# Skewing eight attention heads by a stage in the start of a fused attention and mixture-of-experts kernel

## The chip, the core and the metric

The kernel runs on one core of one Trainium2 chip. The metric is the device time of one execution in microseconds (us). TensorE (PE) multiplies; VectorE (DVE), ScalarE (ACT) and GpSimd (POOL) work on what it leaves; the DMA transfers are issued from one queue, that of SyncE (SP). Each engine takes its instructions in the order in which the program gives them and waits at the first whose inputs are missing.

## The reference

Attention with a decay in the scores, followed by a dense mixture of four experts over all tokens. Batch 4, 8 heads, 576 positions, head size 64; 2304 tokens, model size 512, hidden size 1024.

```python
scores = scale * (q @ k.T)                       # per head
cum = np.cumsum(np.log(np.clip(f, 1e-4, 1)), -1)
scores = where(causal, -1e9, scores + cum[..., :, None] - cum[..., None, :])
attn = softmax(scores)
x = (attn @ v)  ->  tokens x 512
p = domain_probs / domain_probs.sum(-1)
out = sum over e of p[:, e] * (relu(x @ w1[e]) @ w2[e])
```

## The kernel before

Every matrix product is made of float32 operands split into a high part (a float32r copy, written `hi`, `th`, `wh`) and a low part (the rest, `kl`, `tl`, `wl`), so each split costs one copy and one subtraction, and each product two or three passes of TensorE.

The positions of a batch are cut into a first half of 256 rows and a second of 320. A `Job` is one batch, one pair of heads and one half; a head of a job is what the loops run over. The tokens are cut into nine chunks of 256. The experts run as `Step`s, each with a chunk and two 128-wide pieces of a hidden layer; a step needs two weight tiles of 128 x 1024. In the first sweep the first eight steps all use chunk 0, so each of them wants two new weight tiles.

Chunk 0 needs the first halves of all eight heads of batch 0. They are worked in `startup()`, under a manual schedule: the order of the calls is the order on each engine. The loop over `s` runs the heads against one another. For each head the parts are:

- `prep`: the copy `hi` on ACT, a copy of the queries into `q2` on POOL, and two subtractions (into `kl` and into the lower half of `hi`) on POOL (on DVE for the first job);
- `qk_pe` on PE and `qk_min` on DVE: scores, and their masked minimum;
- `qk_exp` on ACT: two exponentials with their sums;
- `tr_pe` on PE, `tr_hi` on ACT, `tr_lo` on DVE: the exponentials transposed and split;
- `av_both` on PE: the product with the values (`prep_v` splits those, on POOL and DVE);
- per pair: `recip` (DVE, and POOL for the copy `rb`), `spread` (PE, and a copy `r` on ACT), and `fin`, which multiplies (DVE), copies to `xh` (ACT) and subtracts into `xl` (DVE).

Into the loop are set `late_sums()` (the decay sums of the second half, on DVE, and their trip through DRAM), the first two weight tiles (`w_split`, after the iterations in `W_SLOT`), and the products of the first step by their four contraction blocks k (`l1_k`, after the iterations in `L1_SLOT`). Below, heads are counted 0 to 7, and k=3 is the last block, which needs the rows of the last pair.

A weight tile arrives by `w_load` in one of the raw slots of `wr_p`; `w_split(n)` copies it to `wh` on ACT and subtracts into `wl` in two halves, on DVE if n is in `W_DVE` (the even n up to 14), else on POOL; the slot is free after that, and the next load can be issued.

After the loop the rest of the program (the second and later heads' work as `asteps`, paced among the steps by `pace`) is put into an order by the compiler's own scheduler.

Of the kernel before, what the change touches and what calls it, by code (L numbers as in the profile page):

```python
# [8 lines left out]
F32 = mybir.dt.float32  # L9
F32R = mybir.dt.float32r  # L10
AF = mybir.ActivationFunctionType
ALU = mybir.AluOpType
# [5 lines left out]
CH = 256  # L18
NCH = NT // CH
NPR = H // 2  # L20
# [9 lines left out]
DIRECT = (0, 1, 2, 3, 4)  # L30
LEAD = 3
W_DVE = tuple(range(0, 16, 2))
W_SLOT = (4, 5)
NEAR = 2
LATE = 6
L1_SLOT = {8: (0, 1), 9: (2,), 10: (3,)}
JOBS = ((0, 0), (1, 0), (2, 0), (3, 0), (0, 1), (1, 1), (2, 1), (3, 1))


# [32 lines left out]
def fused(ctx: ExitStack, tc: tile.TileContext, qk, v, f, probs, w, out):  # L72
    nc = tc.nc
# [12 lines left out]
    xh_p = SB("xh", 4)  # L86
    xf_p = SB("xf", 4)
    w_p = SB("w", 6)
    wr_p = SB("wr", 2)
    g_p = SB("g", 2)  # L90
    acc_p = SB("acc", 4)
    dr_p = ctx.enter_context(tc.tile_pool(name="dr", bufs=4, space=bass.MemoryType.DRAM))
# [20 lines left out]
    def decays():  # L113
        nc.sync.dma_start(out=fr, in_=f)
        first_loads()
        for t in q2:
            nc.gpsimd.memset(t[64:66, :].bitcast(F32), 8.0)
        make_identity(nc, ident)
        for t in [zero] + v4:
            nc.gpsimd.memset(t.bitcast(F32), 0.0)  # L120
        nc.vector.memset(ones, 1.0)
        for c in PARTS:
            nc.vector.tensor_scalar(
                out=fr[:, c], in0=fr[:, c], scalar1=1e-4, scalar2=1.0, op0=ALU.max, op1=ALU.min
            )
            nc.scalar.activation(out=fr[:, c], in_=fr[:, c], func=AF.Ln)
        nc.scalar.activation(out=warm, in_=ones[:, :1], func=AF.Exp)
        sums(0)
        nc.gpsimd.memset(mask, 0.0)
        nc.gpsimd.affine_select(  # L130
            out=mask[:, S - 128 :],
            in_=mask[:, S - 128 :],
            pattern=[[-1, 128]],
            compare_op=ALU.is_ge,
            fill=NEG,
            base=0,
            channel_multiplier=1,
        )
        for h in range(NEAR):
            jobs[0].near(h)  # L140
        for n in range(2):
            nc.sync.dma_start(out=ncd[:, n, :CH], in_=nc2[n][:, :CH].bitcast(F32))
        first_raw(2)
        for j in (0, 2):
            n = 1 if j == 0 else 0
            nc.sync.dma_start(
                out=first_kl[j // 2][64:66, 512 * n :].bitcast(F32).rearrange(
                    "p (h s) -> p h s", s=CH
                ),
                in_=ncd[2 * (j + n) : 2 * (j + 2), :, :CH].rearrange("h n s -> n h s"),  # L150
            )
        first_raw(3)
        w_load(0)
        w_load(1)
        nc.sync.dma_start(out=pr_r, in_=probs)
        jobs[NPR].load()

# [65 lines left out]
    class Job:  # L223
# [76 lines left out]
        def prep_lo(self, hh):  # L300
            if hh not in self.kl:
                self.rows(hh)
            wq, wk, ko, qo = self.wq, self.wk, self.ko, self.qo
            r, hi, kl = self.raw[:, hh, :], self.hi[hh], self.kl[hh]
            eng = nc.gpsimd if self.half == 0 and self is not jobs[0] else nc.vector
            eng.tensor_tensor(
                out=kl[:64, :wk],
                in0=r[:64, ko : ko + wk],
                in1=hi[:64, ko : ko + wk].bitcast(F32),
                op=ALU.subtract,  # L310
            )
            eng.tensor_tensor(  # L312
                out=hi[64:128, qo : qo + wq],
                in0=r[64:128, qo : qo + wq],
                in1=hi[64:128, qo : qo + wq].bitcast(F32),
                op=ALU.subtract,
            )

# [224 lines left out]
        def av(self, hh):  # L543
            self.av_pe(hh)
            self.av_top(hh)
            self.av_add(hh)

        def fin(self):
            w_ = self.wq
            pieces = place(self.b, self.half)  # L550
            k = self.pr
            direct = any(p[1] in DIRECT for p in pieces)
            if self not in jobs[:NPR]:
                self.spread()
            if direct:
                nc.vector.tensor_tensor(  # L556
                    out=self.xs[:, :w_],
                    in0=self.o[:, :w_] if self in jobs[:NPR] else self.xs[:, :w_],
                    in1=self.r[:, :w_],
                    op=ALU.mult,  # L560
                )
            for d, c, o, n in pieces:
                if c in DIRECT:
                    th, tl = x_tiles(c)
                    nc.scalar.activation(
                        out=th[:, k, o : o + n], in_=self.xs[:, d : d + n], func=AF.Copy
                    )
                    nc.vector.tensor_tensor(  # L568
                        out=tl[:, k, o : o + n],
                        in0=self.xs[:, d : d + n],  # L570
                        in1=th[:, k, o : o + n].bitcast(F32),
                        op=ALU.subtract,
                    )
                else:
                    if c not in xf:
                        xf[c] = xf_p.tile([128, NPR, CH], F32, tag="xf", name=f"xf{c}")
                    if direct:
                        nc.gpsimd.tensor_copy(
                            out=xf[c][:, k, o : o + n], in_=self.xs[:, d : d + n]
                        )  # L580
                    else:
                        nc.vector.tensor_tensor(
                            out=xf[c][:, k, o : o + n],
                            in0=self.xs[:, d : d + n],
                            in1=self.r[:, d : d + n],
                            op=ALU.mult,
                        )
# [7 lines left out]
    jobs = []  # L595
# [45 lines left out]
    def w_load(n):  # L641
        if n < NW and n not in wraw:
            wraw[n] = wr_p.tile([128, 1024], F32, tag="wr", name=f"wr{n}")
            nc.sync.dma_start(out=wraw[n], in_=w[n % 32])

    def w_split(n):
        if n >= NW:
            return
        w_load(n)
        wh[n] = w_p.tile([128, 1024], F32R, tag="wh", name=f"wh{n}")  # L650
        wl[n] = w_p.tile([128, 1024], F32R, tag="wl", name=f"wl{n}")
        r = wraw.pop(n)
        nc.scalar.activation(out=wh[n], in_=r, func=AF.Copy)  # L653
        for a in (0, 512):
            z = a + 512
            eng = nc.vector if n in W_DVE else nc.gpsimd
            eng.tensor_tensor(  # L657
                out=wl[n][:, a:z], in0=r[:, a:z], in1=wh[n][:, a:z].bitcast(F32), op=ALU.subtract
            )
        w_load(n + 1)  # L660
        w_load(n + 2)

    acc = {}
    l2 = {}
# [152 lines left out]
    def startup():  # L817

        J = lambda h: heads[h] if 0 <= h < FIRST else (None, None)
        decays()  # L820
        for h in range(2):
            j, hh = J(h)
            j.prep(hh)
        heads[0][0].prep_v()
        for h in range(2):
            J(h)[0].begin(h)
        heads[0][0].qk_pe(0, (0, 1))
        heads[0][0].qk_min(0, 0)
        heads[0][0].qk_min(0, 1)
        for s in range(FIRST + 3):  # L830
            (j, hh), (m, mm), (n, nn), (i, ii) = J(s), J(s + 1), J(s + 2), J(s - 2)
            if n:
                n.begin(nn)
                n.prep_hi(nn)
                n.prep_lo(nn)
            if m:
                m.qk_pe(mm, m.its)
                for t in m.its:
                    m.qk_min(mm, t)
            if j:  # L840
                for t in j.its:
                    j.qk_exp(hh, t)
            if i:
                i.av_both(ii)
            if j:
                j.tr_pe(hh, 0)
                j.tr_hi(hh, 0)
                j.tr_lo(hh, 0)
                if hh == 1:
                    j.recip()  # L850
                if hh == 0 and s > 0:
                    j.prep_v()
            if s >= 2 and s % 2 == 0 and s <= FIRST:
                heads[s - 1][0].spread()
            if s >= 4 and s % 2 == 0:
                heads[s - 4][0].fin()
            if s == LATE:
                late_sums()
            if s in W_SLOT:
                w_split(W_SLOT.index(s))  # L860
            for k in L1_SLOT.get(s, ()):
                if k == 0:
                    steps[0].l1_zero()
                for fi in range(2):
                    steps[0].l1_k(fi, k)
        j = heads[FIRST][0]
        w_split(2)
        j.prep(0)
        w_split(3)
        j.prep_v()  # L870
        j.begin(0)
        normalize()
        for n in range(4, 6):
            w_split(n)
# [71 lines left out]
```

## Time and profile before

| | |
|---|---|
| median of 3 runs | 1033.07 us (1031.91 to 1033.54) |
| profiled execution, its own time | 1033.34 us |
| span of the profiled execution | 1031.6 us |
| busy in the span | PE 97%, DVE 52%, ACT 43%, POOL 32% |
| mean granted clock of TensorE | 0.99 |

The span runs from the first to the last recorded instruction; 1.74 us of the execution's own time lie outside it. All rows below are of that execution. A start and a duration are in us. The bracket behind an instruction gives how long its engine had been idle before it, and what ended that.

### The profile page before, as it was taken

How to read it: one execution, taken by the hardware profiler on the slowest of the kernel's cores; microseconds unless marked ns; L12 is line 12 of the kernel's file. 1: busy time of each engine (PE TensorE's matmuls, PEld its weight loads, DVE VectorE, ACT ScalarE, POOL GpSimd, SP SyncE). 2: the span in 40 equal slices, each digit the busy share in tenths (PEclk: the TensorE clock that was granted, in tenths of full speed). 3: DMA queues.
4: the chain of work that ended last, by engine and by line, in shares of the span. 5: the costliest groups of instructions: out<-in, count | busy, mean ns of one | idle time of the engine just before them, and what ended most of it. 6: DMA issues, size and time to landing. Idle time of an engine off the chain costs nothing.

```text
span 1031.6 us, 16826 instructions
## 1 busy us (share of the span) xinstructions
PE 1003.7 (97%) x6561; PEld 917.3 (89%) x6561; DVE 535.8 (52%) x1181; ACT 447.5 (43%) x897; POOL 326.9 (32%) x357
## 2 busy tenths in 40 slices
PE   4789999999999999999999999999999999999998
PEld 4679899989999999999999999999999999999997
DVE  5667655686867756667566665532222222222222
ACT  5466765566656536455455455422121211212110
POOL 6466876251402204031223144213030311303010
PEclk9699999999999999999999999999999999999999
DMA  5255653342412314022131332211120202102001
GB/s 175 62 183 170 179 151 112 95 160 90 131 50 81 101 49 131 15 91 97 58 123 55 111 118 61 86 59 44 40 82 1 83 19 64 51 32 82 1 21 62
DMA packets 30544, 87.02 MB, mean 84 GB/s; under 512 B 3301, under 2 KB 5537, under 8 KB 30465
## 3 DMA queue, kind: packets, MB, share of 16 engines
q1 hardware_dynamic: 30464, 85.94, 26.5%
q8 instruction: 52, 0.85, 0.3%
q14 instruction: 28, 0.22, 0.1%
HBM read 81.06 MB, written 4.87 MB: 83 GB/s over the span
## 4 chain that ended last, share of the span: by engine, by line
PE 88%; DMA 3%; DVE 3%; ACT 1%; POOL 1%; issue 1%; SPq 0%; ACTq 0%; DVEq 0%; POOLq 0%
PE l L698 37%; PE l L728 36%; PE s L350 5%; PE t L445 5%; PE o L514 4%; DMA wr<-in_w 2%; DMA raw<-in_qk 1%; DVE wl L657 1%; ACT wh L653 1%; PE b L410 1%; POOL wl L657 0%; DVE v L285 0%; DVE hi L312 0%; POOL hi L312 0%; DVE xs L556 0%
## 5 line engine op out<-in xcount | busy, mean ns | idle before, releaser
L657 POOL TENSOR_TENSOR wl<-wr,wh 128x512 fp32r<-128x512 f32 x176 | 228.2, 1325 | 351.9 <-ACT wh L653 348.1
L698 PE MATMUL l<-xh,wh 128*128 128x256 f32 x1152 | 330.6, 287 | 3.1 <-ACT wh L653 3.0
L698 PE MATMUL l<-xh,wl 128*128 128x256 f32 x1152 | 327.9, 285 | 0.7 <-DVE wl L657 0.6
L698 PE MATMUL l<-xl,wh 128*128 128x256 f32 x1152 | 327.9, 285 | 0.1
L710 DVE SCALAR_TENSOR_TENSOR gl<-l,gh 128x512 fp32r<-128x512 f32 x144 | 99.1, 689 | 271.5 <-ACT gh L709 270.7
L728 PE MATMUL l<-wh,gh 128*128 128x512 f32 x576 | 231.1, 401 | 0.0
L698 PEld LDWEIGHTS l<-xh,wh 128*128 128x128 f32 x1152 | 220.8, 192 | 9.2 <-ACT wh L653 4.2
L728 PE MATMUL l<-wl,gh 128*128 128x512 f32 x576 | 227.5, 395 | 0.0
L698 PEld LDWEIGHTS l<-xl,wh 128*128 128x128 f32 x1152 | 220.7, 192 | 5.6 <-DVE xl L568 0.3
L728 PE MATMUL l<-wh,gl 128*128 128x512 f32 x576 | 225.5, 394 | 0.0
L698 PEld LDWEIGHTS l<-xh,wl 128*128 128x128 f32 x1152 | 220.6, 192 | 2.0 <-DVE wl L657 1.1
L709 ACT ACTIVATE gh<-l 128x512 fp32r<-128x512 f32 x144 | 85.5, 595 | 278.5 <-PE l L698 277.5
L379 ACT ACTIVATE p<-p,nm 128x576 f32<-128x576 f32 (+2 forms) x160 | 96.0, 601 | 92.1 <-DVE nm L364 91.7
L653 ACT ACTIVATE wh<-wr 128x1024 fp32r<-128x1024 f32 x96 | 100.0, 1054 | 68.1 <-DMA wr<-in_w 44.7
L728 PEld LDWEIGHTS l<-wh,gl 128*128 128x128 f32 x576 | 108.3, 188 | 23.0 <-DVE gl L710 0.4
L728 PEld LDWEIGHTS l<-wh,gh 128*128 128x128 f32 x576 | 109.1, 189 | 16.2 <-ACT gh L709 0.4
L728 PEld LDWEIGHTS l<-wl,gh 128*128 128x128 f32 x576 | 109.1, 189 | 15.5
L750 DVE SCALAR_TENSOR_TENSOR acc<-l,prob,acc 128x512 f32<-128x512 f32 x126 | 93.9, 748 | 28.8 <-PE l L728 26.1
L364 DVE CUSTOM_DVE_ANT_0 p<-s,mask 128x288 f32<-128x288 f32 (+2 forms) x160 | 75.9, 478 | 52.4 <-PE s L350 51.4
L298 POOL CAST q<-raw 64x320 fp32r<-64x320 f32 (+1 forms) x56 | 27.7, 496 | 226.7 <-PE s L350 208.9
L462 DVE TENSOR_TENSOR ptl<-t,pth 128x320 fp32r<-128x320 f32 (+2 forms) x120 | 65.9, 553 | 63.2 <-ACT pth L455 62.7
L445 PE MATMUL t<-ident,p 128*128 128x128 f32 x480 | 81.5, 279 | 4.0 <-ACT p L379 3.5
(80 smaller groups left out, 1001.5 us busy)
## 6 DMA issues: line engine op xcount, KB each, us to landing
wr<-in_w SPq DMA_DIRECT2D x96, 512.0 KB
raw<-in_qk SPq DMA_DIRECT2D x16, 896.0 KB
raw<-in_qk SPq DMA_DIRECT2D x12, 512.0 KB
vr<-in_v SPq DMA_DIRECT2D x16, 320.0 KB
out<-acc SPq DMA_DIRECT2D x16, 256.0 KB
first<-in_qk SPq DMA_DIRECT2D x4, 512.0 KB
vr<-in_v SPq DMA_DIRECT2D x12, 128.0 KB
first<-in_v SPq DMA_DIRECT2D x1, 512.0 KB
```

What stands on the lines that cost most here:

```text
L350: nc.tensor.matmul(out=ps[:, at : at + z - a], lhsT=lhsT, rhs=rhs, start=(m == 0), stop=(m == 1),)
L364: nc.vector.tensor_tensor_reduce(out=pt[:, a:z], in0=ps, in1=mask[:, m0 + a : m0 + z], scale=-0.125, scalar=BIG if n == 0 else nm[:, col : ...
L379: nc.scalar.activation(out=pt[:, :w_], in_=pt[:, :w_], func=AF.Exp, scale=-1.0, bias=self.nmax[hh][:, c : c + 1], accum_out=self.ssum[:, h ...
L445: nc.tensor.transpose(ps[:, at : at + 128], self.p[hh, it][:, TOK0[jt] : TOK0[jt] + 128], ident)
L462: nc.vector.tensor_tensor(out=lo[:, a0 + first : a0 + at - first], in0=ps[:, 2 * first : at], in1=hi[:, a0 + first : a0 + at - first].bitc ...
L653: nc.scalar.activation(out=wh[n], in_=r, func=AF.Copy)
L657: eng.tensor_tensor(out=wl[n][:, a:z], in0=r[:, a:z], in1=wh[n][:, a:z].bitcast(F32), op=ALU.subtract)
L698: nc.tensor.matmul(out=self.l1p[:, fi, :], lhsT=lhsT, rhs=rhs[:, k, :], start=(k == 0 and m == 0 and not self.whole), stop=(k == 3 and m = ...
L709: nc.scalar.activation(out=self.gh, in_=self.l1p, func=AF.Relu)
L710: nc.vector.scalar_tensor_tensor(out=self.gl, in0=self.l1p, scalar=0.0, in1=self.gh.bitcast(F32), op0=ALU.max, op1=ALU.subtract,)
L728: nc.tensor.matmul(out=l2[tt], lhsT=lhsT, rhs=rhs, start=(self.ps == 0 and fi == 0 and m == 0), stop=(self.ps == 1 and fi == 1 and m == 2),)
L750: nc.vector.scalar_tensor_tensor(out=acc[c][:, tt, :], in0=l2[tt], scalar=sc, in1=acc[c][:, tt, :], op0=ALU.mult, op1=ALU.add,)
```

## The change

The raw weight slots go from two to three, and a third weight tile is asked for at the very start; each `w_split(n)` now also asks for tile n+3. In the loop, each iteration's parts stand in another order: the exponentials of head s first, then the preparation of head s+2, the scores of head s+1, the transposition of head s, and the value product of head s-1 (before: s-2). `fin` of the first four jobs is cut into three calls, which stand in the odd iterations around the exponentials and the scores. The loop has ten iterations in place of eleven. The tiles' splits move (tile 0 stays at iteration 4, tile 1 goes from 5 to 6, tile 2 from behind the loop into iteration 8), `late_sums` goes from iteration 6 to 8, the first step's products start at iteration 7 (before 8). The two subtractions of `prep_lo` change places.

```diff
-W_SLOT = (4, 5)
+W_SLOT = (4, 6)
 NEAR = 2
-LATE = 6
-L1_SLOT = {8: (0, 1), 9: (2,), 10: (3,)}
+L1_SLOT = {7: (0, 1), 8: (2,), 9: (3,)}
...
-    wr_p = SB("wr", 2)
+    wr_p = SB("wr", 3)
...
         w_load(1)
+        w_load(2)
...
+        def fin_mult(self):
+            w_ = self.wq
+            nc.vector.tensor_tensor(
+                out=self.xs[:, :w_], in0=self.o[:, :w_], in1=self.r[:, :w_], op=ALU.mult
+            )
+
+        def fin_hi(self):
+            th, _ = x_tiles(self.b)
+            nc.scalar.activation(out=th[:, self.pr, :], in_=self.xs[:, :CH], func=AF.Copy)
+
+        def fin_lo(self):
+            th, tl = x_tiles(self.b)
+            nc.vector.tensor_tensor(
+                out=tl[:, self.pr, :],
+                in0=self.xs[:, :CH],
+                in1=th[:, self.pr, :].bitcast(F32),
+                op=ALU.subtract,
+            )
...
         w_load(n + 2)
+        w_load(n + 3)
...
-        for s in range(FIRST + 3):
-            (j, hh), (m, mm), (n, nn), (i, ii) = J(s), J(s + 1), J(s + 2), J(s - 2)
+        for s in range(FIRST + 2):
+            (i, ii), (j, hh), (m, mm), (n, nn) = J(s - 1), J(s), J(s + 1), J(s + 2)
+            ends = s % 2 == 1
+            if ends and s >= 3:
+                heads[s - 2][0].fin_mult()
+            if j:
+                for t in j.its:
+                    j.qk_exp(hh, t)
+            if ends and s >= 3:
+                heads[s - 2][0].fin_hi()
             if n:
                 n.begin(nn)
-                n.prep_hi(nn)
-                n.prep_lo(nn)
+                n.prep(nn)
             if m:
                 m.qk_pe(mm, m.its)
                 for t in m.its:
                     m.qk_min(mm, t)
-            if j:
-                for t in j.its:
-                    j.qk_exp(hh, t)
-            if i:
-                i.av_both(ii)
+            if ends and s >= 3:
+                heads[s - 2][0].fin_lo()
             if j:
                 j.tr_pe(hh, 0)
                 j.tr_hi(hh, 0)
                 j.tr_lo(hh, 0)
-                if hh == 1:
-                    j.recip()
-                if hh == 0 and s > 0:
-                    j.prep_v()
-            if s >= 2 and s % 2 == 0 and s <= FIRST:
-                heads[s - 1][0].spread()
-            if s >= 4 and s % 2 == 0:
-                heads[s - 4][0].fin()
-            if s == LATE:
-                late_sums()
+            if i:
+                i.av_both(ii)
+            if ends and j:
+                j.recip()
+                if m:
+                    m.prep_v()
+            if not ends and s >= 2:
+                i.spread()
             if s in W_SLOT:
                 w_split(W_SLOT.index(s))
...
+            if s == FIRST:
+                late_sums()
+                w_split(2)
         j = heads[FIRST][0]
-        w_split(2)
+        w_split(3)
         j.prep(0)
-        w_split(3)
         j.prep_v()
```

## Rows read from the trace of the kernel before

**Rows 1.** The page: busy tenths of TensorE in 40 slices of the span.

```profile
PE   4789999999999999999999999999999999999998
```

**Rows 2.** Two stretches: busy us (count) per engine, granted clock, DMA share, GB/s.

```profile
20.00:30.00 10.00, 6.73 (x40) 5.77 (x41) 6.48 (x20) 6.30 (x20) 6.45 (x14) 0.76 0.05 16
70.00:80.00 10.00, 7.66 (x46) 6.90 (x45) 7.46 (x19) 7.31 (x19) 6.77 (x9) 0.83 0.50 159
```

**Rows 3.** The chain that ended last, 46 to 62 us: start, us, what.

```profile
49.00 3.63 DMA wr<-in_w
...
55.10 5.26 DMA wr<-in_w
```

**Rows 4.** Waits of TensorE, 46 to 200 us: total, times, longest.

```profile
PE l L698 <- ACT wh L653: 3.0, 2, 2.3
...
PE l L698 <- DVE wl L657: 0.6, 1, 0.6
```

**Rows 5.** Timeline of TensorE after its longest wait: start, us, instruction.

```profile
76.67 0.78 PE L728 MATMUL l<-wh,gh 128*128 128x512 f32 x1
...
79.81 0.33 PE L698 MATMUL l<-xh,wl 128*128 128x256 f32 x1
```

**Rows 6.** Timeline of ScalarE, 22 to 31 us.

```profile
22.62 0.39 ACT L379 ACTIVATE p<-p,nm 128x128 f32<-128x128 f32 x1
...
26.94 0.42 ACT L565 ACTIVATE xh<-xs 128x256 fp32r<-128x256 f32 x1 [1.94 <-DVE xs L556]
27.26 1.04 ACT L653 ACTIVATE wh<-wr 128x1024 fp32r<-128x1024 f32 x1
28.21 0.61 ACT L297 ACTIVATE hi<-first 128x512 fp32r<-128x512 f32 x1
28.73 0.39 ACT L379 ACTIVATE p<-p,nm 128x128 f32<-128x128 f32 x1
...
30.48 0.49 ACT L455 ACTIVATE pth_first<-t 128x384 fp32r<-128x384 f32 x1 [0.78 <-PE t L445]
```

**Rows 7.** Timeline of VectorE: weights' low parts, a product of finished rows.

```profile
28.33 1.84 DVE L657 TENSOR_TENSOR wl<-wr,wh 128x512 fp32r<-128x512 f32 x2 [0.52 <-ACT wh L653]
...
36.10 0.41 DVE L556 TENSOR_TENSOR xs<-o,r 128x256 f32<-128x256 f32 x1
...
61.48 2.19 DVE L657 TENSOR_TENSOR wl<-wr,wh 128x512 fp32r<-128x512 f32 x2 [2.05 <-ACT wh L653]
...
68.59 1.29 DVE L657 TENSOR_TENSOR wl<-wr,wh 128x512 fp32r<-128x512 f32 x2 [1.82 <-ACT wh L653]
```

**Rows 8.** Timeline of GpSimd, 24 to 35 us.

```profile
24.71 0.73 POOL L312 TENSOR_TENSOR hi<-first,hi 64x256 fp32r<-64x256 f32 x1
...
32.87 2.50 POOL L657 TENSOR_TENSOR wl<-wr,wh 128x512 fp32r<-128x512 f32 x2
```

**Rows 9.** Timeline of TensorE, 30 to 47 us.

```profile
30.82 0.47 PE L350 MATMUL s<-hi 128*128 128x128 f32 x1 [0.37 <-POOL hi L312]
...
31.83 0.41 PE L493 MATMUL o<-pth_first,v 128*128 128x256 f32 x1
...
33.01 0.86 PE L445 MATMUL t<-ident,p 128*128 128x128 f32 x3
33.66 0.64 PE L410 MATMUL b<-ident,rb 128*128 128x128 f32 x2
33.95 0.56 PE L493 MATMUL o<-pth_first,v 128*128 128x256 f32 x1
...
41.26 0.41 PE L698 MATMUL l<-xh,wh 128*128 128x256 f32 x1
...
43.82 0.41 PE L493 MATMUL o<-pth_first,v 128*128 128x256 f32 x1
...
46.16 0.38 PE L698 MATMUL l<-xh,wh 128*128 128x256 f32 x1
```

**Rows 10.** Timeline of the SP queue, 70 to 78 us.

```profile
71.41 5.52 SPq L264 DMA_DIRECT2D kl<-ncd  x2
```

More of the change, by code (lines that the diff above doesn't have):

```diff
@@ L306, in prep_lo @@
             eng.tensor_tensor(
+                out=hi[64:128, qo : qo + wq],
+                in0=r[64:128, qo : qo + wq],
+                in1=hi[64:128, qo : qo + wq].bitcast(F32),
+                op=ALU.subtract,
+            )
+            eng.tensor_tensor(
                 out=kl[:64, :wk],
@@ L309, in prep_lo @@
                 in1=hi[:64, ko : ko + wk].bitcast(F32),
[L310 to L315, printed above, removed]
                 op=ALU.subtract,
@@ L546, in av @@
             self.av_add(hh)
+        def fin_mult(self):
[12 more added lines that the diff above has]
+                in1=th[:, self.pr, :].bitcast(F32),
+                op=ALU.subtract,
+            )
         def fin(self):
@@ L552, in fin @@
             direct = any(p[1] in DIRECT for p in pieces)
-            if self not in jobs[:NPR]:
-                self.spread()
+            self.spread()
             if direct:
@@ L557, in fin @@
                     out=self.xs[:, :w_],
-                    in0=self.o[:, :w_] if self in jobs[:NPR] else self.xs[:, :w_],
+                    in0=self.xs[:, :w_],
                     in1=self.r[:, :w_],
```

## The prediction

> **What bounds the kernel now.** I read the page's 40 slices first: from the third slice on TensorE is nine or ten tenths busy [rows 1], so the last 950 us are its own work and the change can only take or give what lies before: the start-up loop, and the stretch after it in which the first expert steps run. The stretches by ten microseconds say how these differ. At 20 to 30 us, inside the loop, every engine is busy for 6.3 to 6.7 of 10 us and none is full: a chain of hand-overs sets the pace, and the granted clock is 0.76 on the mean, that is, part of the stretch at 1.2 and part at 2.4 GHz [rows 2]. At 70 to 80 us TensorE loses time again: 7.66 us busy at a clock of 0.83 [rows 2]. The chain that ended last tells why: after the loop it runs through the load of a raw weight tile (3.63 to 5.26 us), its copy on ACT and its subtraction, and round again, because with two slots the next load waits for the subtraction [rows 3]. The waits of TensorE there: 3.0 us in two waits for a `wh` copy, one of them 2.3 us, and 0.6 us for a `wl` [rows 4]. After the long one TensorE ran at 1.2 GHz: from 76.67 to 79.81 us [rows 5]. So two things are to be costed: when the first step's last block (k=3) can start, which was 46.16 us [rows 9], and how much of the weights' lateness goes.
>
> **The skew, A.** No operation is removed; the same heads, copies and products are issued. What changes is which hand-overs lie in a row. In an ordinary iteration the round trip that ACT made through the transposition is covered by the next head's copy. But GpSimd's two subtractions are spaced 0.79 us [rows 8], so that with the query copy and the per-pair work it has over 2 us a head, and I give the first five heads no gain: the exponentials of head 4 start at 22.62 as before [rows 6]. That is where I chose against the change; a gain of up to 0.5 us there is in the range.
>
> From there I add up the longest chain in the new order, with TensorE at 1.2 GHz, as the rows of 30 to 47 us show it. The prices: exponentials 0.97 (28.73 to 29.70, where ACT falls idle), `wh` 0.95 (27.26 to 28.21), `hi` 0.52 (28.21 to 28.73), a 128x256 copy on ACT (`xh`, `r`) 0.32 (26.94 to 27.26) [rows 6]; a product of finished rows on DVE 0.41, a `wl` pair on DVE 1.29 to 1.84 [rows 7]; POOL's two subtractions 1.58 [rows 8]; on PE scores 1.01, value product 1.18, transposes 0.65, spread 0.29, 12 products of the first step 2.56, so six of them 1.28 and the 512-column one that zeroes the bank 0.43 [rows 9].
>
> Iteration 4: exponentials 0.97, transposes 0.65, value product 1.18, spread 0.29, `r` 0.32: 26.0. As the clock is high in part of this stretch, I take 25.7. Tile 0: `wh` 0.95, `wl` 1.29 to 1.84: 27.9 to 28.5. Now the change adds a wait: the first call of iteration 5 on DVE is the product of job 1's rows, behind tile 0's subtraction; behind it wait the `xh` copy on ACT, and behind that, in ACT's order, the copy `hi` of head 7. So 0.41, 0.32, 0.52, POOL 1.58, scores of head 7 1.01: 31.8 to 32.3. Iteration 6: transposes, value product, spread, `r`, 2.44, and tile 1's `wh` 0.95, which stands before head 7's exponentials on ACT: 35.2 to 35.7. Exponentials 0.97, transposes 0.65, value product 1.18, zeroing 0.43, 12 products 2.56, value product of head 7 1.18, spread 0.29: 42.4 to 43.0. Tile 2 is the second such place: `r` 0.32, `wh` 0.95, `wl` 1.29 to 1.84 stand before the last pair's product of rows on DVE, then 0.41 and 0.32: 45.7 to 46.8. Twelve hand-overs at about 0.05 each add 0.6. So k=3 starts at 46.3 to 47.4; I take 46.9, 0.7 later than before. One iteration fewer is thus eaten by the splits inside the chain.
>
> The price of one `wl` pair decides half a microsecond at each of two places. The rows show 1.29 us where GpSimd was idle, 1.84 where it started a subtraction midway, 2.19 where it ran two or more beside it [rows 7]. The Trainium skill, SBUF — State Buffer, section "SBUF: two separate sides", says that VectorE with two SBUF inputs and GpSimd take a shared port pair as a whole, and the one that comes second is blocked until the other ends; the spread from 1.29 to 2.19 agrees. By the free price the chain ends at 46.3, with 2.19 at both places at 48.1.
>
> What else the gap before k=3 does: TensorE finishes block k=2 1.28 us after the spread, at 44.0, and then has nothing until 46.9, a gap of about 2.5 to 3 us. Before, there was none. A wait of 2.3 us is in the trace, and after it TensorE spent 3.14 us at 1.2 GHz (76.67 to 79.81), which loses half of that, 1.57 us [rows 4, 5]. I put the same here. A is +0.7 + 1.6 = **+2.3 us** (bounds: -2.2 if the upper clock holds throughout, +3.5 with both contended subtractions).
>
> **The third slot, B.** Tile 2 is already in SBUF when its split comes; the start's extra load stands before the probabilities and head 8's raw data on SP, and at 20 to 30 us the DMA engines are nearly idle (share 0.05) [rows 2], so nothing behind it gets late. Tile 4 is asked for when tile 1 is done (before 40 us, not 49.0), tile 6 when tile 3 is done (about 51, not 55.10) [rows 3]. With a load of 3.63 to 5.26 us these come 4 us or more ahead of before, and the longest wait to be covered is 2.3. Each later load has one more tile's time of slack. So I let the waits go: 3.0 + 0.6 [rows 4], and with the long one its stretch at 1.2 GHz, 1.57 [rows 5]: B is **-5.2 us** (bounds: -2.6 if every second wait stays, -6 if smaller gaps close too).
>
> **Nothing:** the swapped subtractions (the scores need both), the cut of `fin` (the same three instructions), `late_sums` in iteration 8 (DVE waits for tile 2's `wh` there), the third load request of a split (it waits on SP for the same subtraction as the second did before).
>
> Sum, on the profiled execution's own 1033.34 (span 1031.6 and 1.74 outside): 1033.34 + 2.3 - 5.2 = **1030.4 us**. The median of the runs is 0.27 us lower.
>
> **The rivals.**
>
> *The skew works as well* (0.21). If TensorE keeps 2.4 GHz through the loop, its terms in the chain, some 11 us from iteration 4 on, halve in the parts after 25 us: 4.5 us less, k=3 at 42.4, 3.8 ahead of before; with the 1.6 for the last gap: 1033.34 - 3.8 + 1.6 - 5.2 = 1025.9. For it: the engines' loads leave room. Against: with every engine below 7 of 10 us the clock fell, and the new order leaves TensorE as many gaps around tiles 0 and 1.
>
> *The weights stay late* (0.18). SP serves in order, and a `kl` load held it from 71.41 for 5.52 us, in two issues, until a score buffer came free [rows 10]; a third slot doesn't help a load behind that. Half of B: 1033.34 + 2.3 - 2.6 = 1033.0, no change.
>
> *Slower* (0.17). Tile 3's subtraction on POOL (2.50 us [rows 8]) now stands before head 8's preparation, and tile 5, landing earlier, may stand before head 9's. If the scheduler has put those scores among the first steps' products as early as before, TensorE waits for POOL: 2.5 for each, 1033.34 + 2.3 - 5.2 + 5.0 = 1035.4. It decides once more than 2.9 us of such waits are there. For it: PE takes its order strictly. Against: the scheduler knows POOL's order too.
>
> The forecast itself has 0.44.
>
> **How the numbers follow.** 0.2%, 2 us, is about what a measurement of this kernel can tell from no change; against 1033.07 faster is below 1031.0, slower above 1035.1. The forecast at 1030.4, give or take 2.5: 0.27 faster, 0.15 same, 0.02 slower. The first rival: 0.21 faster. The weights' rival: 0.02, 0.14, 0.02. Slower: 0.04 same, 0.13 slower. Sum: faster 0.50, same 0.33, slower 0.17. The range takes in both outer rivals to their middle: 1025.5 to 1035.5; the forecast's own is 1028 to 1033.
>
> **What would show it.** Right: k=3's first product at 46.3 to 47.4 us with an idle stretch of TensorE of over 2 us ahead of it, ended by ACT's `xh` behind DVE; a granted clock of 0.5 there; no wait of TensorE for `wh` over 0.5 us after 50 us, and a clock of 1.0 at 70 to 80. Wrong: k=3 before 44 (the first rival); waits for `wh` still over 1.5 us in sum (the second); waits of PE's scores for POOL after 50 us (the third). If the compiler's order of the rest costs TensorE idle time beyond 140 us, none of the cases has it, and the prediction fails there.

## The result, and the profile after

The changed kernel is slower: 1041.37 us (median of four runs, 1039.68 to 1042.45) against 1032.49 in the same job, a ratio of 1.0084 with a 95% interval of 1.0065 to 1.0102. That is 8 to 9 us, outside the range of the prediction and on the side that it thought least likely. The profiled execution took 1042.11 us, its span 1040.3, 8.7 more than before.

First the 40 slices of the page, TensorE's row, to be laid beside [rows 1]:

```profile
PE   5789999999998999999999999999999999999998
```

Behind the first slice (5, before 4) there is one new digit: the 8 in the thirteenth slice, at 312 to 338 us. This is the stretch of which the prediction said that TensorE's own work sets the pace. The windows of the changed kernel, with the columns of [rows 2], give it sizes:

```profile
20.00:30.00 10.00, 7.66 (x36) 6.24 (x35) 5.22 (x18) 6.55 (x20) 5.25 (x11) 0.68 0.20 72
50.00:60.00 10.00, 7.17 (x43) 5.86 (x42) 9.83 (x14) 6.24 (x11) 8.85 (x10) 1.00 0.44 135
60.00:70.00 10.00, 8.19 (x56) 7.29 (x55) 5.18 (x15) 5.36 (x13) 6.72 (x8) 1.00 0.75 231
70.00:80.00 10.00, 10.00 (x67) 9.08 (x67) 7.99 (x14) 6.56 (x17) 6.74 (x9) 1.00 0.65 198
300.00:400.00 100.00, 97.12 (x638) 88.39 (x637) 70.33 (x169) 57.03 (x118) 17.42 (x23) 0.98 0.23 72
```

and two of these windows in the kernel before, which the rows ahead of the prediction didn't hold:

```profile
50.00:60.00 10.00, 10.00 (x63) 8.74 (x62) 7.74 (x22) 6.56 (x16) 6.81 (x8) 1.00 0.74 236
300.00:400.00 100.00, 100.00 (x677) 92.45 (x676) 68.97 (x161) 54.70 (x109) 23.82 (x26) 1.00 0.26 83
```

I count as lost what a window has beyond busy time times granted clock; it holds idle time and half speed alike. 70 to 80 us lost 3.64 before and nothing after: the third slot's gain is there. But 50 to 60 went from 0 to 2.83, and 300 to 400 from 0 to 4.8 (2.88 idle, 1.9 at the lower clock). From 20 to 50 us, the start itself, the loss is nearly what it was: 13.9 before, 14.3 after. Over all windows from 20 to 1025 us it grows from 20.1 to 27.1; the other 1.7 of the 8.7 I can't place by windows.

The four largest waits of TensorE in the changed kernel, 46 to 140 us (total, times, longest):

```profile
PE l L747 <- DVE gl L729: 3.3, 2, 2.3
PE o L514 <- DVE xs L574: 1.5, 3, 0.6
PE o L514 <- DVE ptl L462: 1.4, 1, 1.4
PE l L717 <- ACT wh L671: 0.8, 1, 0.8
```

and the three largest of the same kernel from 300 to 400 us:

```profile
PE t L445 <- ACT p L379: 1.2, 1, 1.2
PE t L445 <- DVE xs L574: 0.7, 1, 0.7
PE t L445 <- DVE nm L364: 0.5, 1, 0.5
```

The 3.0 us for `wh` of [rows 4] have shrunk to 0.8. In their place TensorE waits for `gl` and for attention work. None of these new waits is for an operation that the diff changes; what has changed is what stands ahead of it. VectorE's timeline of the changed kernel around the longest one (start, us, instruction):

```profile
50.06 2.07 DVE L285 TENSOR_TENSOR v<-vr,v 128x128 fp32r<-128x128 f32 x2 [1.25 <-ACT v L284]
...
53.22 1.81 DVE L675 TENSOR_TENSOR wl<-wr,wh 128x512 fp32r<-128x512 f32 x2
54.96 1.27 DVE L729 SCALAR_TENSOR_TENSOR gl<-l,gh 128x512 fp32r<-128x512 f32 x2
```

and of the kernel before:

```profile
51.66 0.68 DVE L710 SCALAR_TENSOR_TENSOR gl<-l,gh 128x512 fp32r<-128x512 f32 x1
...
53.75 1.29 DVE L657 TENSOR_TENSOR wl<-wr,wh 128x512 fp32r<-128x512 f32 x2 [0.68 <-ACT wh L653]
```

Before, the first `gl` of step 0 stands ahead of tile 4's `wl`, after behind it. TensorE waits 2.3 us for it. The order behind the start is the compiler's scheduler's, and it has made a new one: with the TensorE products of the two traces laid side by side (6561 records in each, compared by names and shapes), 1813 places hold another product. 85 of them are in the start, 1701 lie between 51 and 355 us, 27 behind that.

### The profile page after: what moved, and what is told of

It is laid out like the page before. It is cut to its first block, busy times and chain, and to the rows that moved or that the text cites. A ratio compares the mean times of both kernels' runs of the same rounds, so it can differ in the third digit from the quotient of the medians.

```text
span 1040.3 us, 16837 instructions
## 1 busy us (share of the span) xinstructions
PE 1008.7 (97%) x6561; PEld 919.7 (88%) x6561; DVE 542.3 (52%) x1181; ACT 448.0 (43%) x897; POOL 322.5 (31%) x357
## 4 chain that ended last, share of the span: by engine, by line
PE 90%; DVE 4%; ACT 2%; issue 2%; DMA 1%; POOL 0%; SPq 0%; ACTq 0%; DVEq 0%
PE l L717 38%; PE l L747 37%; PE s L350 5%; PE t L445 5%; PE o L514 4%; PE b L410 1%; DMA wr<-in_w 1%; ACT wh L671 1%; PE o L493 1%; DVE wl L675 1%; DVE v L285 1%; ACT hi L297 0%; DVE acc L769 0%; DVE gl L729 0%; DMA kl<-ncd 0%
```

## The experiments

Three theories stand in the expectations. **S**: the slot costs, since early tiles are subtracted ahead of step 0's `gate`, and VectorE and GpSimd collide. **L**: the new order of the loop costs. **R**: neither does; any edit lets the scheduler lay out the rest of the program anew, and the new layout costs. Each ratio below is to the kernel before in the same job (its median was 1032.65 to 1032.97 in these).

**The slot alone (e1) and the skew alone (e2).** e1 is the kernel before with

```diff
-    wr_p = SB("wr", 2)
+    wr_p = SB("wr", 3)
         w_load(1)
+        w_load(2)
         w_load(n + 2)
+        w_load(n + 3)
```

and e2 the changed kernel with these three undone.

> The old order of the loop, with the three raw slots and the early load of tile 2 alone. Theory S (the slot costs): tiles that land early are subtracted at once, tile 4 ahead of step 0's gate on VectorE and tiles 3 and 5 on GpSimd beside VectorE's value subtractions; TensorE waits 2 to 5 us in 45 to 70 us and the gain at 70 to 80 us (3.9 us) is used up: 1033 to 1038 us. Theory L (the loop's order costs, the slot gains as predicted): 1027 to 1029 us. Theory R (any change lets the scheduler lay out the rest anew, and the new layout costs): 1033 or more, with over 2 us of idle TensorE beyond 140 us.

> The new order of the loop with the two raw slots of before. Theory L: last block at about 48 us, no gain from the slot, the stalls at 60 to 80 us back: 1041 to 1045 us. Theory S: only the loop's 2.2 us remain: 1034 to 1036 us, and step 0's gate stands ahead of tile 4's subtraction on VectorE again. Theory R: over 2 us of idle TensorE beyond 140 us here too.

Measured: e1 1038.08 us, ratio 1.0050 (1.0034 to 1.0065); e2 1039.03 us, 1.0056 (1.0034 to 1.0077). Both parts lose by themselves, which neither S nor L alone explains. R had asked for over 2 us of idle TensorE beyond 140 us in both: from 140 to 600 us e1 has 3.4 us, e2 3.6, the kernel before 0.5. In e1 the third slot does what the prediction said of it, and the loss is elsewhere:

```profile
70.00:80.00 10.00, 10.00 (x74) 9.43 (x74) 8.51 (x20) 8.62 (x20) 5.68 (x7) 1.00 0.68 221
300.00:400.00 100.00, 97.00 (x642) 88.28 (x640) 70.72 (x167) 55.75 (x114) 21.91 (x25) 0.98 0.25 77
```

The loop of e1 is untouched, and it has the stall at 300 to 400 us too, so the stall isn't the new loop's. What e1 shares with the changed kernel there is the third slot and the order: from 250 us on TensorE's products stand in the same places in both traces. p2, below, has the slot without that order, and no stall there.

**Tile 2's split behind the loop again (e3); step 0's gate by hand in the start (e4).** Both are the changed kernel, with

```diff
# e3
             if s == FIRST:
                 late_sums()
-                w_split(2)
         j = heads[FIRST][0]
-        w_split(3)
+        w_split(2)
         j.prep(0)
+        w_split(3)
# e4
         w_split(3)
+        steps[0].gate()
...
-            cur.gate()
+            if n > 0:
+                cur.gate()
```

> The changed kernel, with tile 2 split behind the loop as before instead of ahead of the last pair's rows. The prediction's step: last block 2.2 to 2.8 us earlier, at 45.3 to 46.3 us. Theory L: the end moves with it, 1038 to 1039 us. Theory S: the orders of tile 4 and the gate stay as in the changed kernel, so the time stays within 1 us of 1041.

> The changed kernel, with step 0's gate put into the hand-written order right behind tile 3's split, so that its subtraction stands ahead of the value split and of tile 4 on VectorE. Theory S: the wait of 2.3 us of TensorE for the gate goes, and with it 2 to 4 us: 1037 to 1039 us. Theory L: nothing, 1041 us. Theory R: anything, with idle TensorE elsewhere.

Measured: e3 1040.02 us, 1.0064 (1.0047 to 1.0082); e4 1039.92 us, 1.0069 (1.0044 to 1.0094). Both intervals overlap that of the changed kernel. e4 shows what becomes of the 2.3 us for `gl` (its profiled execution was the shortest of five, 1036.75 us):

```profile
50.00:60.00 10.00, 9.93 (x70) 9.12 (x69) 8.50 (x15) 3.72 (x9) 7.27 (x6) 1.00 0.68 215
60.00:70.00 10.00, 6.06 (x27) 4.80 (x26) 6.98 (x15) 7.23 (x17) 6.83 (x9) 0.83 0.58 204
```

The wait is gone from 50 to 60, and a worse one stands at 60 to 70, where TensorE waits 2.5 us for a `pth` copy on ACT. In this layout, which the scheduler drew anew, mending the one wait gave nothing that the intervals can tell; what it is worth by itself isn't shown.

**The swap of two subtractions alone (n1).** The smallest part of the diff, which the prediction put under "Nothing": the kernel before with the `kl` subtraction of `prep_lo` behind the one into `hi`, for every head, and nothing else.

```diff
-            eng.tensor_tensor(out=kl[:64, :wk], ...)
             eng.tensor_tensor(out=hi[64:128, qo : qo + wq], ...)
+            eng.tensor_tensor(out=kl[:64, :wk], ...)
```

> The kernel before, with one edit of the change alone: the two subtractions of prep_lo change places, the same work on the same engine. It changes the place of about 1270 of TensorE's 6563 products. Theory R: the start takes the same time to 0.5 us, and the whole is 2 us or more away from before, with idle TensorE at 80 to 140 or 300 to 330 us. Theories S and L: no change, within 1 us of before.

Measured: 1041.52 us, 1.0086 (1.0069 to 1.0102). This one swap, of two operations of like size of which the scores need both, costs as much as the whole change. By the count used above, 1606 places of TensorE's order hold another product, all between 49 and 355 us (the 1270 of the expectation stands in no trace). Its windows:

```profile
50.00:60.00 10.00, 8.93 (x54) 7.43 (x53) 8.60 (x19) 6.35 (x17) 6.77 (x8) 1.00 0.70 216
100.00:120.00 20.00, 16.37 (x103) 14.16 (x102) 14.40 (x27) 12.93 (x30) 16.20 (x18) 1.00 0.50 167
200.00:300.00 100.00, 98.35 (x653) 89.31 (x652) 79.07 (x176) 60.70 (x129) 30.40 (x35) 1.00 0.33 111
```

TensorE is idle for 3.63 us at 100 to 120 us (before: 1.23), 1.65 at 200 to 300 (before: 0.50) and 1.07 at 50 to 60 (before: none), and not at all at 300 to 400: another layout, with other holes, for the same loss.

**The layout held fixed (p1, p2, p4, p8).** Here the rest, behind the start, is pinned: on TensorE, ScalarE, VectorE and GpSimd each instruction must follow the one that it followed in the kernel before. SyncE's queue is left free. The edit is the same for all, and only the order that it names differs:

```python
def pin(nc, tc, started):
    rest = nc.cur_bb.bb.instructions[started:]
    for name in ['PE', 'Activation', 'DVE', 'Pool']:
        ...
        for a, b in zip(at, at[1:]):       # at: the order of the kernel before
            tc.add_manual_dep(made[b], made[a].name, ...)   # no semaphore
```

p1 is the changed kernel so pinned, p2 is e1, p4 is e2, p8 is n1. The traces show that the pin holds on TensorE: in p2 and p8 its products stand in the order of the kernel before throughout, in p1 and p4 all but those 85 places of the start.

> The changed kernel, with the instructions behind the start pinned, on TensorE, ScalarE, VectorE and GpSimd, to the order in which they stand in the kernel before. Theory R (the new layout of the rest costs some 4 to 5 us, most of it at 300 to 330 us): that stall goes, 1035 to 1037 us. Theory S or L (the start and the slot cost all of the 8.9): within 1.5 us of 1041.

> Slots alone (old order of the loop), the rest pinned to the order of the kernel before. Theory R: the gain of the slot that was forecast is seen, less the 2.3 us of the gate behind tile 4: 1029 to 1032 us. Theory S: 1036 to 1038 as without the pin.

> The new order of the loop alone, two slots, the rest pinned to the order of the kernel before. Theory R: only the start's own cost is left, 2 to 4 us over before: 1034.5 to 1036.5 us. Theory L: 1039 as without the pin.

> The kernel before with the two subtractions swapped, as in the run of the swap alone, but everything behind the start pinned to the order of before. R: the swap itself costs nothing: 1032 to 1034 us, against 1041.5 with the scheduler's own layout. If the swap itself is what costs (the second half of a copy standing first on its engine), the time stays at 1039 to 1042 us.

| ratio (95% interval) | the scheduler's layout | the layout of before |
|---|---|---|
| swap alone (n1, p8) | 1.0086 (1.0069 to 1.0102) | 1.0016 (1.0007 to 1.0025) |
| slot alone (e1, p2) | 1.0050 (1.0034 to 1.0065) | 0.9960 (0.9945 to 0.9976) |
| skew and swap (e2, p4) | 1.0056 (1.0034 to 1.0077) | 1.0015 (1.0005 to 1.0025) |
| the whole change (after, p1) | 1.0084 (1.0065 to 1.0102) | 0.9998 (0.9985 to 1.0011) |

All four rows fall by 0.4 to 0.9%, 4 to 9 us, with the operations and the start unchanged. R holds: most of each loss belongs to the layout. p2 beats both kernels: 1028.29 us. Two windows of p2, beside those of e1, show that the idle time at 300 to 400 us goes and the third slot's gain at 70 to 80 stays:

```profile
70.00:80.00 10.00, 10.00 (x69) 9.18 (x69) 8.39 (x21) 9.06 (x23) 7.01 (x9) 1.00 0.56 188
300.00:400.00 100.00, 100.00 (x674) 92.35 (x673) 68.61 (x160) 56.10 (x111) 26.63 (x28) 1.00 0.26 80
```

and so do two windows of p8, to be laid beside n1's (idle 1.28 us against 3.63, and 0.48 against 1.65):

```profile
100.00:120.00 20.00, 18.72 (x128) 16.78 (x126) 12.70 (x33) 14.49 (x34) 18.15 (x21) 1.00 0.56 158
...
200.00:300.00 100.00, 99.52 (x675) 91.86 (x674) 77.78 (x182) 62.92 (x130) 28.94 (x33) 1.00 0.32 104
```

**The layout alone (p7).** The converse: the kernel before, its own start and two slots, the rest pinned to the order that the scheduler gave the changed kernel.

> The kernel before with its own start, two slots and its own order among the first eight heads, but everything behind the start pinned to the order that the scheduler gave the changed kernel. R: the layout carries the loss by itself: 1036 to 1040 us, with the idle time of TensorE at 300 to 330 us back. S and L: no slot is added and no order among the first heads is changed, so 1032 to 1034 us.

Measured: 1052.1 us, 1.0175 (1.0157 to 1.0194). The side is R's, the size is not: it is 12 us more than R named. Windows of p7:

```profile
60.00:70.00 10.00, 7.24 (x40) 6.17 (x39) 4.55 (x10) 5.47 (x10) 5.14 (x7) 0.85 0.51 156
200.00:300.00 100.00, 97.78 (x651) 89.67 (x650) 69.34 (x169) 59.43 (x129) 32.39 (x39) 0.98 0.34 107
300.00:400.00 100.00, 96.90 (x644) 87.57 (x643) 73.97 (x177) 55.89 (x118) 17.57 (x23) 1.00 0.26 81
```

The stall at 300 to 400 us is back, with 3.1 us idle, and there are more: an order drawn up for weights that come by three slots is served here by two. So this run says that an order pinned to a kernel can cost by itself, and that pinning alone makes no kernel fast, but not how much of its 18 us is the layout and how much the misfit.

**Two attempts inside the pinned layout (p5, p6).** In p1, whose profiled execution was the shortest of ten (1029.76 us), TensorE has new waits, of which the first two rows between 40 and 200 us are

```profile
PE s L350 <- POOL hi L306: 3.0, 1, 3.0
PE s L350 <- POOL kl L312: 0.9, 1, 0.9
```

and GpSimd's timeline in p1 shows what stands ahead:

```profile
47.63 2.56 POOL L675 TENSOR_TENSOR wl<-wr,wh 128x512 fp32r<-128x512 f32 x2 [7.77 <-ACT wh L671]
50.14 0.46 POOL L298 CAST q<-raw 64x256 fp32r<-64x256 f32 x1
50.67 0.72 POOL L306 TENSOR_TENSOR hi<-raw,hi 64x256 fp32r<-64x256 f32 x1
```

That is the prediction's third rival, tile 3 ahead of head 8's preparation. p5 puts that back in p1; p6 writes step 0's gate by hand in p2:

```diff
# p5
-        w_split(3)
         j.prep(0)
+        w_split(3)
# p6
         w_split(2)
+        steps[0].gate()
```

> The changed kernel with the rest pinned to the order of before, and one part of the skew undone: the preparation of head 8 stands ahead of the third slot's split again. R with the rival of the prediction (GpSimd's subtraction of tile 3 stands ahead of head 8's preparation): the waits of TensorE on POOL hi (3.0 us) and on kl (0.9 us) that the pinned changed kernel shows between 40 and 60 us go, and the time falls from 1032.9 to 1029 to 1031 us. If the order of the tail doesn't matter, the time stays within 1 us of 1032.9.

> The kernel before with three slots and the early load, the rest pinned to the order of before, and step 0's gate written by hand right behind tile 2's split. R: the waits on gl (1.7 us) and gh (0.6 us) behind the start go, and the time is 1026 to 1027.5 us against 1028.3 without the hand-written gate. If the gate only moves the wait to another tile, 1028 to 1029.

Measured: p5 1035.47 us, 1.0019 (0.9999 to 1.0040); p6 1030.5 us, 0.9975 (0.9965 to 0.9985). Neither gains. In p5 the wait for `hi` is gone and that for `kl` is 0.2 us, but the gate, behind it, is now late; its waits, 46 to 140 us:

```profile
PE l L747 <- DVE gl L729: 3.7, 1, 3.7
PE o L514 <- DVE ptl L462: 1.6, 1, 1.6
PE l L747 <- ACT gh L728: 1.0, 1, 1.0
```

In p6 the waits for `gl` and `gh` (1.7 and 0.6 us in p2) are gone as well, and 50 to 60 us is 8.80 busy against 7.65, but smaller waits came for `p` (0.7), `wl` (0.5) and `ptl` (0.5), and the interval overlaps p2's. The gains that were expected of both didn't come.

## Why the prediction was wrong

**What bounds the kernel: the step that failed.** The prediction said that "the last 950 us are its own work and the change can only take or give what lies before". That is so for one given order of instructions. The same prediction noted that the program behind the start is ordered by the scheduler, and its sum left that order as it was. It named the exception in its last sentence (idle time of TensorE beyond 140 us, which none of its cases had), gave it no chance, and that is the case that came: 4.8 us lost at 300 to 400, beside 2.8 at 50 to 60.

**"Nothing: the swapped subtractions": wrong as made, nearly right in itself.** Priced at 0, the swap measured +8.9 us (1.0086) with a new layout and +1.6 us (0.7 to 2.6) with the old one. Whether that last 1.6 is the swap or the pinning isn't told apart: the unchanged kernel was not run pinned to its own order.

**B, the third slot: right.** -5.2 us predicted, bounds -2.6 to -6; with the layout held, -4.1 us (p2, 0.9960, -2.5 to -5.7). The window from 70 to 80 us is full at a clock of 1.00 in the changed kernel, in e1 and in p2, as the prediction's last part asked.

**A, the skew: inside its bounds, but not by its terms.** +2.3 predicted, bounds -2.2 to +3.5; p4, which has swap, skew and pinning together, measures +1.5 (0.5 to 2.6), and as p8 measures the same without the skew, the skew itself is near 0. Block k=3 was to start at 46.3 to 47.4 us. In the profiled execution of p1, which was a short one, it starts at 46.66; the changed kernel's timeline of TensorE has it 1.0 us past the upper end:

```profile
48.41 0.50 PE L717 MATMUL l<-xh,wh 128*128 128x256 f32 x2 [0.29 <-ACT xh L556]
```

The start of the two is one and the same order. The changed kernel is 0.5 us behind p1 already at the scores ahead of iteration 4's transposes (23.37 against 22.89), with the clock still high in both; the runs don't say why. Then TensorE's clock falls at another point of the work: by the windows of two microseconds it is 0.50 from 24 us on in the changed kernel, and 0.89 in p1 at 24 to 26, as the same product of iteration 4 shows in TensorE's timelines. The changed kernel:

```profile
25.85 0.41 PE L493 MATMUL o<-ptl_first,v 128*128 128x256 f32 x1
```

and p1:

```profile
24.60 0.28 PE L493 MATMUL o<-ptl_first,v 128*128 128x256 f32 x1
```

In e4, which reached the same scores at 21.90, the clock is still 1.00 at 26 to 28 us, and k=3 starts at 44.33. The term "as the clock is high in part of this stretch, I take 25.7" is where this sits: that copy `r` ended at 25.93 us in p1 and at 27.88 in the changed kernel. The gap of 2.5 to 3 us before k=3 was not there either. The scheduler put step 1's products into it from 46.30, with waits of 0.77, 0.22 and 0.29 us; the 1.6 for half speed behind the gap falls away.

**The rivals.** The third, GpSimd's subtraction of tile 3 ahead of head 8's preparation, is real where the layout is held: 3.0 + 0.9 us in p1, against 2.5 priced. Slot and skew don't add up: p2 and p4 sum to -2.6 us, close to the forecast's -2.9, but p1, which has both, measures -0.2 (-1.5 to +1.1). The gap of 2.4 us is little more than the noise of the three; it would fit this rival, but p5 took the wait away and got no time back, so its price is not shown. Among the waits of the changed kernel itself, after 46 us, there is none for that preparation. Of the first rival, the skew that works as well, the chip showed at most e4's early k=3 (44.33, its sign was before 44), not its time; the second, late weights, is ruled out by the 0.8 us for `wh`.

**What stays open.** Why the scheduler draws another layout after a swap of equals; no run looks into its costs. Why the whole change gains nothing even with the old layout, where the slot alone gains 4.1 us. Nor is it shown that the order of before is good: it is better in the four pairs above.

## What to carry to other kernels

Where a scheduler orders the rest of a program, an edit has two prices, its own and that of the new layout, and the second can be the larger one in places that the diff doesn't touch. Compare the order of instructions before reading a wait, and hold it fixed to measure an edit; a null edit (a swap of equals) tells how large the second price can be: here as large as the whole change's loss. And where the time is to be kept, pin the layout: the third slot was a loss of 0.5% without it and a gain of 0.4% with it.

## What the runs showed of the hardware

VectorE's small subtractions swelled beside GpSimd's: over 46 to 140 us the 128x128 ones into `v` took 500 ns on the mean before and 1139 after; the pair at 50.06 took 2.07 us while GpSimd worked on a `wl` from 49.39 to 51.98, where a pair before took 0.48 us (54.96) with GpSimd idle. The Trainium skill, SBUF — State Buffer, section "SBUF: two separate sides", says that VectorE with two SBUF inputs and GpSimd take a shared port pair as a whole, so that the one that comes second is blocked. The pair, which ends just behind GpSimd's `wl`, fits it.

The granted clock of a window isn't always the speed. In p2's profile 30 to 40 us stands at 1.00, yet its product of 256 columns takes as long as in p6, where the same window says 0.50. TensorE's timeline of p2:

```profile
35.58 0.41 PE L494 MATMUL o<-ptl_first,v 128*128 128x256 f32 x1
```

and of p6:

```profile
35.20 0.41 PE L494 MATMUL o<-ptl_first,v 128*128 128x256 f32 x1
```

Against the 0.28 us of p1 above, both ran at the lower level. I take the clock from durations where the two differ, and no loss of p2's start is counted from that column.
